# Gated linear attention and a PReLU MLP on one core: level products in pairs, keys and outputs kept in the decay tile, and a new order

## Chip, core and metric

The kernel runs on one core of a Trainium2 chip. The metric is the device time of one execution in microseconds, over several executions; the median is quoted. A profile of one further execution gives the time of every instruction. Engines are named as in the profile: PE is the matrix engine (PEld its weight loads), DVE the vector engine, ACT the scalar engine, POOL the general engine, and SP the engine whose queue issues the DMAs.

## What is computed

The input is four batches of eight heads, 768 tokens, 48 features a head. A complex decay per token and feature is limited in size, a running state of 48 x 48 per head is decayed and increased by key times value at each token, and the query reads its real part. The result goes through a two-layer MLP with a leaky activation.

```python
scale = np.minimum(mag, 0.999) / (mag + 1e-06)
a_re_n, a_im_n = (a_re * scale, a_im * scale)
for t in range(S):
    ar, ai = (a_re_n[:, :, t, :, None], a_im_n[:, :, t, :, None])
    new_re = ar * S_re - ai * S_im
    new_im = ar * S_im + ai * S_re
    S_re, S_im = (new_re + kv, new_im)
    y[:, :, t] = np.einsum('bhd,bhde->bhe', q[:, :, t], S_re)
...
h = x @ w_in                                             # 3072 x 384 by 384 x 2048
g = np.maximum(h, 0.0) + alpha * np.minimum(h, 0.0)
return (g @ w_out).astype(np.float32)
```

## The kernel before

**Units.** The attention is cut into 24 units: four batches of six chunks of 128 tokens, all eight heads at a time. The magnitudes of the decays and their phases are separated. For each unit there is a tile KQ (96 x 2 x 8 x 128: real and imaginary part of the feature on the partitions, queries and keys, heads, tokens), a tile PP of phases, and a tile T of products of decays (96 x 8 x 256). Gates (line 221 on) make phases and decays for one to three chunks at a time with long chains of DVE, ACT and POOL work, and send them to DRAM; a load brings them back in the units' layout.

**Levels.** Inside a chunk the pairs of tokens are taken in six levels, h = 1, 2, 4, 8, 16, 32: each level pairs the second half of every block of 2h tokens with its first half, and a product of queries and keys is needed for it. Between the levels a "step" (line 701) multiplies half of KQ with decays of T, in place, 1,024 elements per partition. So before each level's product, KQ stands in another state.

**One unit, in its order.** L648 multiplies KQ with the phases (2,048 elements, in place). Then, for each level: ACT copies the keys' first halves to W (L719; not for h = 1, whose keys are read with a stride), PE makes the level's product (L662: 16 small matmuls into the PSUM tile ps_lv, of which there are two), DVE steps KQ (L701), and the product is masked into a tile A (L686 on DVE for h up to 8, L683 on ACT for 16 and 32). A step may not begin before the level's product has read KQ. After the last step PE transposes the keys (L736), ACT copies them to KT (L738), PE makes the state increments (L747) and the outputs of all levels from A and the values (L759 and L768), DVE carries the state over two half chunks (L777 and L780, with decays from the last columns of T), PE adds the carried state's part to the outputs (L793), and ACT copies the outputs to yT (L807), which two DMAs (L812) write to DRAM (ysc).

**MLP.** The tokens form 14 groups of one chunk (the first two and the last two) or two chunks. For a group, xT is loaded from ysc. For each of 16 blocks of 128 hidden features PE makes three matmuls (L841), ACT and DVE apply the activation (L848 and L850), and PE adds the block to the output sum (L860, one matmul for each chunk).

**Order and queues.** Every part of the work is a generator. The string ORDER names, letter by letter, which generator goes on next (A to I gates, J to O loads and weights, P to Z and a to m the units, n and o the MLP), and each engine runs its instructions exactly in the order in which they were emitted. So PE, DVE, ACT and SP are in-order queues: an instruction that waits holds up all that stand behind it on its engine. All DMAs are issued by SP. The planner's costs in the code have no effect when the kernel is built.

**Buffers that matter here.** KQ has three buffers, PP one, T two, W two, KT one, yT one, the values V and VL one each. T of a unit comes free after the second L780 of that unit; T of the unit two later is loaded by two DMAs (L593).

Of the kernel before, what the change touches and what calls it, by code (L numbers as in the profile page):

```python
# [30 lines left out]
    "AAAAAAAAAABBAMMABMAAAAAMNAAAMMAAAAAAAAABKAAAAAAJKBBNBAKJANAAAJONNAAAAAAOBNOAAAAAAAAAAAJAAAKKAAAAAAKK"  # L31
    "KBABKLMAMKKKAAAAAAAAAAAAABBAAAAAAAAAALLLNLNOBBBBBBBBBBBBBBBOKKLJBBJBCOCNBBBBNNBBBNNNKNBBNNBBBBBOPBBO"
    "BBOOBBBBBBBLLBBBBBPCPPBBBBBBBBBBBOBJBBBBCBBBNBCBBJBPMMJBLBBBLBOPBLMLJJJPPBBCLBOBONOPBBMCCCCCPNPPCLCN"
    "CCCNNCCOPPKJCPCCJMPPJJJJPCNCOCCCCCCCCPOOOOCCCONNNPPQQCOCMCMDPPPPPPPPPPPPPPPPPNPPCNCNCCCNCPONPOCCCQCN"
    "NPKCQCCCPCPCJQQQPQQQCCCCOCCCCQCPNOJQQCOJDJPJJPPKQPDDONJDQCCCCCCCCCQCCOOCQCDQQOLOCCCCCCCDKMRnQQQMKQQK"
    "KKNCKOKOCCCCKMRJQoOCCQQQQNQoJCDQoCCOCLOCCNCCQONLoooLLLDLLDNNDLLDoooDDLoRoNLoRDoRNNDRDRooLLNRJRRDDDDD"
    "NQRoRQKoQQQRDKDJQEREoDONJDDDMDDDQooooDoDooooooRQooooooQooEDoooDoRRRRoooOooOOooooooDRRRJRoJDSooooooRD"
    "RoRRLooQQooELoSOOOLLLLLLLDDDLLLRQQQSRRKKoLDEooSoQooOoDRooRooLoSoDoooEDDooRoooRRROSRRRREoooooQRREDDDD"
    "SDDDDDDoDEESJJSJEEQDJJRJJJSKSSSTSDDLLLRRRRRRLLLESSSDLLTSDEnToTDDSTSETTSSSSLSJTSSSLLDDDDDDDDEEDDDDooS"
    "LLLoKTSooJSoEooSEoDDDDSEETSSSSSSJJSSSSETTTDJEEETDJooEEEEoUTJJJJLLoEooEEJTooDSoooooEoooTDDDTDoSSSSSoL"  # L40
    "LLLLLLooooUTooULLooEooooULJETDTooDooooooDDTDUoooTTooooLooDUoDooKLTTDooooTToooooDDDTETToUUoooTooToTTT"
    "TTnoDoooooooooTLLLUUoooKooLLLLLUTUoLooLooFEJLTUUUULoooooEoJUEooooooUUUUUUEJooEULEEooooooooUoTKEEEToo"
    "EEUVoTToTUUoEoooVVoooooEooooooVUJVVoUFoVUUooTVoUVVUVEUUJJJJUEEEEEEEEEEEEUoUJJTLTVUVFVoVoFWooFVJVVooo"
    "VFooooUUUVVVJUWVKVVUVWWoooooVLLWLLLLLWLLEEEEEEEEEEEEEEEELVVoVLLoWWoLJVVoWoVUoVWVVVooEooooJEEUWWWoVVV"
    "VWVVVVoWWJJJJJJXooEFnFooEEoEELLLLLLLLKJEFLoooVEoooEEooLEooWLLLWXoWLooooWWEoooEooooKEXEWWWKoVVooooooo"
    "KXooEooooXWJWJXXoooWooooWWFoVVoWVXWooooooWWFXFWWWFEWWFFFFGFXooLJLLLLLLXWooooooWFWFXXJFoooFooooFWoFXX"
    "oLLFoGooooJJooooooJFoWFXXXFWFFFWFFFoFooWFoXFFWXooooooFooooooooooXXXXYooooooooGJFWWFXXFXYooFFoooXLLXX"
    "LFFooooooooooLoooYXGLoooXJoooooGYXXFXXFFXXXXXFFFFFFFJYYFJnYJXoGYoooooJFFFFFFFFFFFFFFFLFJJYZFoooooooL"
    "ooGoYZYXXXGJYYZooXooZZoGoooooYooYXoFooooYYYYYYYYYZZoooZFZFFFooooFXJYZoLLLoYoYJYoLLLLLLLKYoYoYooZGLLY"
    "YKYYYYJFYZYYJKXFFFGGooYYJYLLLJLFFLoooooaFFFoYLFFFoFoJJJooZLFZYYYGYYaGLoLLoLLooooooooFLLFoFFFoooooooo"  # L50
    "ooooZoooaZaJZaoooGoZaJZnGZZZZZaooooooooooooaaooaGaZZoooaooZoJoooJGoZZooZoZoooZaHZZZGGoGGGGGGGZZZZZGZ"
    "GaZKKHLGGGoooooaGGoooooooGooobooGoaoooaoaaaaaoooLoGGbooobbZaaaoaaZooaJZZZLJoLLLLLLLLLLoGGGGaaoooGboG"
    "GJoooZaJJoabboooooooaaaaaaaaGHJZHGJJbbbbGGGLGGooooooHoooobaobJJaGGGGGGGGaaaooJJboocooooooobbcoGGbcHb"
    "ooGbLJJKooooooooooooocbGbHcHcLGLcGGKooooooLLbHbLcbbaabGGGGGGooooobbKcGbGJGJGcLLGGGooooHGGcobbbcHoooo"
    "bbLooooLLLLbbbnbcGHbbbbbJGGGdoooooGoLLoocbGGGGGccbooooJJboooGKobGGoGHooLLLLLLoooGHbbbboLooooooooGcLL"
    "LdddccccHdooooocccooooooocdcccdooJoddoLoooooHJcdocLHdJoHdHKHdcoJJooooooocccccIIccoccceooJJooHLLLoooo"
    "oooLoLdeLcHHcccHHHHccccoLLLHHLHHHHnooHoHHHLooooooooHJooooeIdLLLooooooooddooooooeeeHHHHdooHoHHdHeeooo"
    "oooooodddddeooooooodJdoJoeooHHHHHHHHHHHoodoodododeoododooodeedddddddHHdHHHHHHIeeKKeeKHJJooJfooooIooo"
    "ooeeeKeddfoLLdeeooeoeoooJooLooooddLLHHHHHHHHHHHHHHJeedIeeeLfooLLoLLooefLLLLeIofdooeeeHHeeeeeeHHefIIf"
    "IfHfJHHJHJdJooooooeeJJJJJeeeoeegLJHLHHLLofoLLLLLLLofIoooooooooIHooLJffooJoHoooooHogofHoHHIoooooIoooo"  # L60
    "noffoHHooooogfoofoooooffIffffLgoogoooofgooLoffIfJoofoIfIIooJoIfoofooooffffffffffgKggooooohLLLooLhogo"
    "oIoLgghgoooooJJILLLoooLLLffILLfhIIIgghoooooooooohgooJJhgfJJfhhKffggIgggKgooohoooohhggggJghooohoogogo"
    "IgIgooooggIgggggggIhJhoLLgLgIIIIJgIogooooKKoIoooIhooLooILhIoooooooggKJIIIIIIIIJJoooooiLIhoooIIIIoIoo"
    "oooihnooIhhhhihhiooooIiooooLLLLLLiihhLLohohoooooohohohoooohhIIIIhhIhhhhhhJJJIooooooooooJJLiioihiioio"
    "JIoLooLiiijoooooIIIooooIIIioIIIIIIIIIIoiiiiiihhhhhjLLhjLoLLLLLLLiJIIIIIIIoooooojooooojoiijjjoooiooio"
    "jiiooooiLhIIIIIoIoioiiiiiiJLLLLLILooooooLLoooiIioooiiiiiIijjoIiiiIIooooooooooooonJooJJJJooojjjjooooo"
    "ooooooooooooJoLLjjoojojjoojoLkojLjjoooooooooojjkokoooooojjkkjookkoooojjjooLooooLjkjjjjJkkooojjkjjkoo"
    "oooJoooooooookJJokjjJJLllLooLokLkoLoLLLjjkkLkkkLLLLLkkjJjjkooooooooooooJkollkokkJoooooooooookllllooj"
    "kokooJJJlJokoooookkkkJkkkkkkkkkllLLlkLLooomkkkoooolooooooLollooooolloJooomloooonoooooooooooooooooooo"
    "oooooooooollllJlmmooooooooooolmmlooooooolllooolLLLLolomLLLLLllooooooooollloolmlmmmmoooooooomlllloooo"  # L70
    "ooooooooooomlmlmlmoolommllllnoooooooooooooommLmmmoooooooooooooooooooooooooomoLomLooooomommoLLLLLoooL"
    "LLmmmLLooooooooooooooooooooooooooooooooooooooooooommmmmmmmmoommmmmoooooomnoooooooooooooooooooooooooo"
# [30 lines left out]
def kernel(  # L103
# [46 lines left out]
    LEVELS = [1 << i for i in range(6)]  # L150
# [16 lines left out]
    masks, by_row = {}, {}  # L167

    def mask(h):

        m = work.tile([P, P // h, h], F32, tag="W", name="mask", bufs=2)
        nc.gpsimd.memset(m, 1.0)
        nc.gpsimd.affine_select(out=m, in_=m, pattern=[[-h, P // h], [0, h]], base=0,
                                channel_multiplier=1, compare_op=ALU.is_ge, fill=0.0)
        nc.gpsimd.affine_select(out=m, in_=m, pattern=[[h, P // h], [0, h]], base=h - 1,
                                channel_multiplier=-1, compare_op=ALU.is_ge, fill=0.0)
        masks[h] = consts.tile([P, HC], F32, tag=f"mask{h}", name=f"mask{h}")
        flat = m.rearrange("p n h -> p (n h)")
        for i in range(2):
            nc.gpsimd.tensor_copy(masks[h][64 * i:64 * i + 64],  # L180
                                  flat[64 * i:64 * i + 64, HC * i:HC * (i + 1)])


    for h in (16, 32):
        by_row[h] = []
        for m in range(HC // h):
            t = consts.tile([P, 1], F32, tag=f"rows{h}_{m}", name=f"rows{h}_{m}")
# [8 lines left out]
    def step(*args, **kwargs):  # L196
# [5 lines left out]
        KQ=3, PP=1, T=2, V=1, W=2, KT=1, St=3, yT=1, xT=2, raw0=1, raw1=1, raw2=1, g0=0, g1=0, g2=0, ot=2, top=2,  # L202
# [7 lines left out]
    bias_tiny = consts.tile([P, 1], F32, tag="bias_tiny")  # L210
    nc.vector.memset(bias_tiny, TINY)
    bias_one = consts.tile([P, 1], F32, tag="bias_one")
    nc.vector.memset(bias_one, ONE)
    bias_two = consts.tile([P, 1], F32, tag="bias_two")
    nc.vector.memset(bias_two, 2.0)
    bias_plus = consts.tile([P, 1], F32, tag="bias_plus")
    nc.vector.memset(bias_plus, 2.0 ** -100)
    bias_half = consts.tile([P, 1], F32, tag="bias_half")
    nc.vector.memset(bias_half, -0.5)

    def gates(g, b, c0, c1):
# [136 lines left out]
        run = work.tile([P, 2, NK, GT // L // Rn + 1], F32, tag="run", name="run", bufs=2)[:, :, :, 0:nr + 1]  # L358
        ends = runs = work.tile([P, 3, NK * GT // L // Rn], F32, tag="runs", name="runs", bufs=2)[:, :, 0:rows]

        def three(dst, re_im, k, t):

            yield ACT(1.5 * k, t)
# [9 lines left out]
        t = yield from three(ends, blk[:, :, Rn - 1], 2 * rows, t)  # L373
# [18 lines left out]
        for o in range(2):  # L392
# [4 lines left out]
            tiny_engine.tensor_tensor(out=offv[:, o, 1:Rn], in0=m[:, 0], in1=m[:, 1], op=ALU.add)  # L397

# [13 lines left out]
        begin = work.tile([P, 2, NK], F32, tag="begin", name="begin", bufs=2)  # L412
# [149 lines left out]
    def loads():  # L562
        for u in range(NU):
# [24 lines left out]
            for i in range(2):  # L588
                rows = slice(i * D, (i + 1) * D)
                t = yield DMA(393, ("T", u), takes=() if i else (R["T"],))  # L590
                if i == 0:
                    L["T"] = T = work.tile([D2, H, TL], F32, tag="T", name="T", bufs=2)
# [43 lines left out]
    KT = consts.tile([P, H * D2 + P - D2], F32, tag="KT")  # L636
    nc.gpsimd.memset(KT[:, H * D2:], 0.0)
    nothing = KT.bitcast(BF16)[:, 2 * H * D2:2 * H * D2 + D]

# [3 lines left out]
    def unit(u):  # L643
        b, c = divmod(u, NCH)
        r = yield DVE(2 * H * P, ("KQ", u), ("rotation", u))
        L = loaded[u]
        KQ, PP = L["KQ"], L["PP"]
        nc.vector.tensor_tensor(out=KQ, in0=KQ, in1=bass.AP(  # L648
            tensor=PP.tensor, offset=PP.offset, ap=[PP.ap[0], (1, 2), (P + 1, H), (1, P)]), op=ALU.mult)
# [3 lines left out]
        def meet(h, weights, *after):  # L653

            e = yield PE(0.28, *after, *[("met", h, u - 1)] * (u > 0), takes=(R["lv"], R[h]), mode=1, n=16)
# [297 lines left out]
```

## Time and profile before

| what | us |
|---|---|
| median of three executions (lowest, highest) | 863.18 (861.69, 864.44) |
| the profiled execution | 859.8 |
| its span, first to last instruction | 858.1 |
| PE busy, 11,488 records | 704.7 |
| DVE busy, 996 records | 655.6 |
| ACT busy, 913 records | 427.1 |
| steps L701, 144 of 1,248 ns | 178.3 |
| phase products L648, 24 of 2,292 ns | 55.0 |
| key copies L719, 120 of 623 ns | 74.3 |
| level products L662, 4,608 records | 68.5 |
| copies to KT L738, 48 of 479 ns | 23.0 |
| copies to yT L807, 96 of 366 ns | 32.0 |

The times of the profile are those of one execution, so sums made from them are set against its own time and not against the median. Records of one engine overlap at their ends, so that the mean of one instruction is longer than what it adds to its engine's busy time. An fp32 matmul leaves two records. What bounds the end is a matter of stages, not of the totals: no engine is busy for the whole span.

### The profile page before, as it was taken

What the parts mean: (1) busy time and instruction counts of PE and PEld (TensorE: products, weight loads), DVE (VectorE), ACT (ScalarE), POOL (GpSimd) and SP (SyncE); (2) the same over time, 40 slices, a digit from 0 to 9 for tenths busy, and PEclk for the clock granted to TensorE, in tenths of its full rate; (3) what the DMA queues carried; (4) which work ended last, traced back from release to release, by engine and by line L of the source; (5) the groups of instructions that cost most, each with busy time, mean ns of one, the idle gap of its engine ahead of it and who ended that gap; (6) DMA issues with size and microseconds to landing.
All of it is one profiled execution on the core that took longest, in us unless ns stands there. A gap on an engine that the chain in (4) does not pass through costs nothing.

```text
span 858.1 us, 26855 instructions
## 1 busy us (share of the span) xinstructions
PE 704.7 (82%) x11488; PEld 529.1 (62%) x11488; DVE 655.6 (76%) x996; ACT 427.1 (50%) x913; POOL 186.3 (22%) x293
## 2 busy tenths in 40 slices
PE   0000414976898999999999999999999999999998
PEld 0000313655676777777777777777777777777776
DVE  5999999999976899789978987798867665444212
ACT  7757578576434565554555554654334234233221
POOL 5212323457313200440034005300052000000000
PEclk9999965896999999999999999999999999999999
DMA  7689977977688778669684787865674766221110
GB/s 222 170 211 232 269 175 178 241 154 154 170 194 165 159 195 207 125 135 227 160 182 110 180 216 147 158 170 127 176 155 74 173 121 134 63 51 38 39 39 9
DMA packets 194559, 130.92 MB, mean 153 GB/s; under 512 B 74504, under 2 KB 186248, under 8 KB 194440
## 3 DMA queue, kind: packets, MB, share of 16 engines
q1 hardware_dynamic: 194440, 129.20, 64.9%
q8 instruction: 90, 1.47, 0.8%
q14 instruction: 29, 0.24, 0.1%
HBM read 100.82 MB, written 35.71 MB: 159 GB/s over the span
## 4 chain that ended last, share of the span: by engine, by line
PE 74%; DVE 15%; SPq 3%; issue 3%; DMA 3%; ACT 2%; DVEq 0%; ACTq 0%
PE ps_o L860 29%; PE ps_h L841 29%; PE ps_lv L662 5%; PE ps_y L768 4%; DVE KQ L701 3%; PE ps_kv L747 3%; PE ps_y L793 3%; SPq L556 2%; DVE gate L336 2%; PE ps_kt L736 2%; DMA V<-in_v_dram 1%; DVE gate L338 1%; DVE gate L316 1%; DVE gate L296 1%; DVE gate L422 1%
## 5 line engine op out<-in xcount | busy, mean ns | idle before, releaser
L841 PE MATMUL ps_h<-xT,w_in_sb 128*128 128x256 f32 (+1 forms) x1344 | 303.4, 357 | 0.0
L860 PE MATMUL ps_o<-w_out_sb,g_sb 128*128 128x384 f32 x768 | 297.5, 501 | 7.2 <-DVE g_sb L850 7.1
L841 PEld LDWEIGHTS ps_h<-xT,w_in_sb 128*128 128x128 f32 x1344 | 233.8, 193 | 69.9 <-issue 1.7
L701 DVE TENSOR_TENSOR KQ<-KQ,T 96x1024 f32<-96x1024 f32 x144 | 178.3, 1248 | 44.1 <-PE ps_lv L662 41.1
L848 ACT ACTIVATE g_sb<-ps_h 128x256 f32<-128x256 f32 (+1 forms) x224 | 78.9, 353 | 235.8 <-PE ps_h L841 235.1
L850 DVE SCALAR_TENSOR_TENSOR g_sb<-g_sb,al,ps_h 128x256 f32<-128x256 f32 (+1 forms) x224 | 97.5, 437 | 126.8 <-ACT g_sb L848 126.4
L860 PEld LDWEIGHTS ps_o<-w_out_sb,g_sb 128*128 128x128 f32 x768 | 137.4, 192 | 58.0 <-DVE g_sb L850 9.7
L662 PE MATMUL ps_lv<-KQ,W 96*32 96x32 f32 x3840 | 56.5, 205 | 57.5 <-ACT W L719 54.1
L719 ACT COPY W<-KQ 96x512 f32<-96x512 f32 x120 | 74.3, 623 | 55.4 <-DVE KQ L701 54.1
L662 PEld LDWEIGHTS ps_lv<-KQ,W 96*32 96x32 f32 x3840 | 44.6, 116 | 83.0 <-ACT W L719 62.4
L662 PE MATMUL ps_lv<-KQ 96*32 96x32 f32 x768 | 12.0, 206 | 68.2 <-DVE KQ L648 52.6
L511 POOL TENSOR_SCALAR top<-top 128x768 f32<-128x768 f32 x16 | 43.5, 2721 | 84.3 <-ACT top L503 84.0
L648 DVE TENSOR_TENSOR KQ<-KQ,PP 96x2048 f32<-96x2048 f32 x24 | 55.0, 2292 | 0.0
L662 PEld LDWEIGHTS ps_lv<-KQ 96*32 96x32 f32 x768 | 9.5, 119 | 71.8 <-DVE KQ L648 52.6
L336 DVE TENSOR_TENSOR gate<-gate 128x576 f32<-128x576 f32 (+5 forms) x84 | 48.3, 575 | 3.1 <-ACT gate L308 1.3
L768 PE MATMUL ps_y<-A,VL 64*48 64x64 f32 x2304 | 42.2, 223 | 8.6 <-issue 6.8
L683 ACT ACTIVATE A<-ps_lv,rows 128x64 f32<-128x64 f32 x144 | 39.2, 331 | 19.4 <-PE ps_lv L662 19.0
L336 POOL TENSOR_TENSOR gate<-gate 128x72 f32<-128x72 f32 x42 | 19.0, 451 | 127.2 <-ACT gate L366 124.4
L768 PEld LDWEIGHTS ps_y<-A,VL 64*48 64x48 f32 x2304 | 39.6, 125 | 11.0 <-issue 8.9
L422 DVE TENSOR_TENSOR gate<-gate 128x1152 f32<-128x1152 f32 (+2 forms) x36 | 43.5, 1233 | 0.1
L807 ACT COPY yT<-ps_y 48x256 f32<-48x256 f32 x96 | 32.0, 366 | 21.1 <-PE ps_y L793 20.4
L686 DVE TENSOR_TENSOR A<-ps_lv,mask 128x256 f32<-128x256 f32 x96 | 39.5, 414 | 0.0
(100 smaller groups left out, 774.5 us busy)
## 6 DMA issues: line engine op xcount, KB each, us to landing
T<-decs SPq DMA_DIRECT2D x48, 384.0 KB
PP<-phs SPq DMA_DIRECT2D x48, 193.5 KB
KQ<-in_q_dram SPq DMA_DIRECT2D x48, 192.0 KB
decs<-gate SPq DMA_DIRECT2D x7, 1152.0 KB
phs<-gate SPq DMA_DIRECT2D x14, 576.0 KB
KQ<-in_k_dram SPq DMA_DIRECT2D x40, 192.0 KB
vsc<-in_v_dram SPq DMA_DIRECT2D x48, 144.0 KB
VL<-vsc SPq DMA_DIRECT2D x24, 288.0 KB
```

What stands on the lines that cost most here:

```text
L336: on(4 * k).tensor_tensor(out=m, in0=w[:, 1::-1].unsqueeze(2).to_broadcast([P, 2, 2, k]), in1=pairs_of(u), op=ALU.mult)
L422: TT(out=m[:, a], in0=U5[:, 1 + a], in1=turned(off3, o)[:, a].unsqueeze(1).unsqueeze(3).to_broadcast([P, L // 2, nb, 2]), op=ALU.mult)
L511: nc.gpsimd.tensor_scalar(out=top, in0=top, scalar1=F64_SMALL, scalar2=None, op0=ALU.max)
L648: nc.vector.tensor_tensor(out=KQ, in0=KQ, in1=bass.AP(tensor=PP.tensor, offset=PP.offset, ap=[PP.ap[0], (1, 2), (P + 1, H), (1, P)]), op=A ...
L662: nc.tensor.matmul(t[64 * i + j:64 * i + j + HC // 2, p], lhsT=weights(4 * i + p)[:, j:j + HC // 2], rhs=q_[:, m * g:m * (g + 1)], start=T ...
L701: nc.vector.tensor_tensor(out=x, in0=x, in1=m, op=ALU.mult)
L719: nc.scalar.copy(W.rearrange("p n t -> p (n t)").rearrange("p (m h) -> p m h", h=h), halves(KQ[:, 1].rearrange("p n t -> p (n t)"), h)[:, ...
L768: nc.tensor.matmul(o, lhsT=Vp[h][64 * i:64 * i + 64, s, e_ * D:(e_ + 1) * D], rhs=a, start=False, stop=False)
L841: nc.tensor.matmul(p, lhsT=w_in_sb[:, f // 2, kk, f % 2 * P:(f % 2 + 1) * P], rhs=x_of[m][:, kk], start=(kk == 0), stop=(kk == NK - 1))
L848: nc.scalar.activation(gt, p, AF.Relu, scale=-1.0)
L850: nc.vector.scalar_tensor_tensor(out=gt, in0=gt, scalar=al_1[:, f:f + 1], in1=p, op0=ALU.mult, op1=ALU.add)
L860: nc.tensor.matmul(sums[0], lhsT=gt[:, c * P:(c + 1) * P], rhs=w_out_sb[:, f], start=(f == 0), stop=(f == NF - 1))
```

## The change

**Pairs.** The levels are visited in pairs (1, 2), (4, 8), (16, 32). The first level of a pair is made from a copy of both its halves, queries' and keys' (tile WQ, of which there are two), so that its step waits for the copy and no longer for the product. For h = 1 there is no extra copy: the phase product is split in two of 1,024 elements, and the one for the half concerned writes straight into WQ (L665 of the changed kernel), from which step 1 then writes KQ. For h = 4 and 16 ACT copies 1,024 elements (L744). For h = 2 and 8 ACT copies the keys as before; for h = 32 the keys are read in place. Both products of a pair go into one PSUM tile, and the two masks follow after the second step of the pair.

**Tiles.** KT and yT are gone. T has 128 partitions; its first 128 columns, done with after step 1, take the transposed keys (two copies each, the second one filling the gap from column 96 to 128), and after the state increments the outputs. T therefore comes free when the outputs of the unit have been written to DRAM. The small constant columns share one tile, a small zero tile takes the place of KT's zero columns, and some buffers of the gates (run, runs, begin) are single instead of double.

**Order.** ORDER is new as a whole.

```diff
-    LEVELS = [1 << i for i in range(6)]
+    VISITS = [(1, 2), (4, 8), (16, 32)]
+    LEVELS = [h for visit in VISITS for h in visit]
...
-        r = yield DVE(2 * H * P, ("KQ", u), ("rotation", u))
...
-        nc.vector.tensor_tensor(out=KQ, in0=KQ, in1=bass.AP(
-            tensor=PP.tensor, offset=PP.offset, ap=[PP.ap[0], (1, 2), (P + 1, H), (1, P)]), op=ALU.mult)
+        def some(at, q_to_k):
+
+            return bass.AP(tensor=KQ.tensor, offset=KQ.offset + at, ap=[KQ.ap[0], (H * P + q_to_k, 2), (P, H), (2, HC)])
+
+        def phases(at, q_to_k):
+
+            return bass.AP(tensor=PP.tensor, offset=PP.offset + at, ap=[PP.ap[0], (q_to_k, 2), (P + 1, H), (2, HC)])
+
+        first_slot = spare.pop(0)
+        WQ = work.tile([D2, 2, H, HC], F32, tag=f"WQ{first_slot}", name="WQ", bufs=1)
+        nc.vector.tensor_tensor(out=WQ, in0=some(1, -1), in1=phases(1, 0), op=ALU.mult)
+        r = yield DVE(H * P)
+        nc.vector.tensor_tensor(out=some(0, 1), in0=some(0, 1), in1=phases(0, 2), op=ALU.mult)
...
-        def meet(h, weights, *after):
-
-            e = yield PE(0.28, *after, *[("met", h, u - 1)] * (u > 0), takes=(R["lv"], R[h]), mode=1, n=16)
-            t = ps.tile([P, HP, HC // 2], F32, tag="lv", name="ps_lv", bufs=2)
+        def meet(h, shared, at, keys, queries, *after, takes=()):
+
+            e = yield PE(0.28, *after, *[("met", h, u - 1)] * (u > 0), takes=takes, mode=1, n=16)
+            if not shared:
+                shared.append(ps.tile([P, 2, HP, HC // 2], F32, tag="lv", name="ps_lv", bufs=2))
+            t = shared[0][:, at]
...
-        for h in LEVELS:
-            w = k_
-            if h == 1:
-                weights = lambda n: KQ[:, 1, n].rearrange("p (m s) -> p m s", s=2)[:, :, 0]
-            else:
-                w = yield ACT(H * HC, k_, takes=(R["W"],))
-                W = work.tile([D2, H, HC], F32, tag="W", name="W", bufs=2)
...
-            e, t = yield from meet(h, weights, w, k_)
...
-            k_ = yield DVE(2 * H * HC, e, *[("decays", u)] * (h == 1))
-            T = L["T"]
-            step(h)
-            yield from mask_out(h, t, e)
+        for visit in VISITS:
+            ready = []
+            for h in visit:
...
+                elif h != visit[-1]:
+                    held = "WQ"
+                    w = yield ACT(2 * H * HC, k_, takes=(R[held],))
+                    slot = spare.pop(0)
+                    z = work.tile([D2, 2, H, HC], F32, tag=f"WQ{slot}", name="WQ", bufs=1)
+                    nc.scalar.copy(z.rearrange("p i n t -> p i (n t)").rearrange("p i (m h) -> p m i h", h=h), bass.AP(
+                        tensor=KQ.tensor, offset=KQ.offset + h, ap=[KQ.ap[0], (2 * h, H * HC // h), (H * P - h, 2), (1, h)]))
...
+                if h != visit[-1]:
+                    k_ = yield DVE(2 * H * HC, w, *[("decays", u)] * (h == 1))
+                    T = L["T"]
+                    step(h, WQ if h == 1 else None)
+            tiles, shared = [], []
+            for at, (h, keys, queries, held, slot, w) in enumerate(ready):
+                e = yield from meet(h, shared, at, keys, queries, w, k_, takes=() if at else (R["lv"],))
...
+            if visit[-1] != 1:
+                k_ = yield DVE(2 * H * HC, e)
+                step(visit[-1])
+            for h, ta, e in tiles:
+                e = yield from mask_out(h, ta, e)
...
-            nc.scalar.copy(KT[:, 4 * i * D2:4 * (i + 1) * D2].rearrange("p (n d) -> p n d", n=HP), t)
+            nc.scalar.copy(T[:, 4 * i:4 * (i + 1), 0:D2], t)
+            nc.scalar.copy(T[:, 4 * i:4 * (i + 1), D2:P], t[:, :, 0:P - D2])
...
-        R["T"].put(k_)
...
-                    yT = work.tile([P, 2, 2, P], F32, tag="yT", name="yT", bufs=1)
+                    yT = T[:, 0:4, 0:P].rearrange("p (i s) t -> p i s t", i=2)
...
-                              yT[64 * e_:64 * e_ + D].rearrange("p i s t -> p (i s) t"))
-        R["yT"].put(t)
+                              T[64 * e_:64 * e_ + D, 0:4, 0:P])
+        R["T"].put(t)
```

## The prediction

> **What bounds the kernel now.** I read the page's totals and 40 slices first, then the windows by stage, then who waited for whom, then the timeline of one level product. The slices show two regimes:
>
> ```profile
> PE 704.7 (82%) x11488; PEld 529.1 (62%) x11488; DVE 655.6 (76%) x996; ACT 427.1 (50%) x913; POOL 186.3 (22%) x293
> ...
> PE   0000414976898999999999999999999999999998
> ...
> DVE  5999999999976899789978987798867665444212
> ...
> PEclk9999965896999999999999999999999999999999
> ```
>
> A slice is 21.5 us. DVE is full from the second slice to the eleventh while PE fills; from about the fourteenth on PE is full. The windows put numbers on it (columns: length, busy time and instructions of PE, PEld, DVE, ACT, POOL, granted clock, DMA share, GB/s):
>
> ```profile
> 141.00:205.00 64.00, 45.73 (x945) 34.62 (x945) 62.75 (x88) 42.96 (x79) 34.06 (x33) 0.77 0.75 180
> 205.00:250.00 45.00, 39.17 (x788) 29.98 (x787) 38.86 (x59) 17.96 (x49) 12.46 (x18) 0.94 0.80 187
> 250.00:307.00 57.00, 52.84 (x961) 40.34 (x959) 46.25 (x59) 31.21 (x76) 15.49 (x34) 0.97 0.79 158
> ...
> 360.00:858.00 498.00, 493.91 (x7353) 367.37 (x7351) 335.04 (x470) 208.75 (x507) 74.86 (x140) 1.00 0.56 125
> ```
>
> Up to 205 us DVE sets the pace, after 307 PE does, and in the 102 us between neither is full: DVE idles 17. Its waits there (from 205 to 307: us, times, longest), and what PE waits for meanwhile:
>
> ```profile
> DVE g_sb L850 <- ACT g_sb L848: 7.8, 6, 3.7
> DVE KQ L701 <- PE ps_lv L662: 7.2, 4, 4.0
> ```
>
> ```profile
> PE ps_y L768 <- issue: 6.0, 3, 2.7
> ```
>
> Over the whole run DVE waits 41.1 us for level products, but 33.1 of it after 307, where DVE has time to spare. So the change is not worth 41 us.
>
> A ledger of the two queues follows. Both engines run their instructions in a fixed order. I gave each DVE instruction the time its kind adds to DVE's busy time here (a 1,024-element step 1.19 us net of overlap), and each matmul its spacing, start to start, between 300 and 858 us (L860 0.653, L841 0.436 for two chunks and 0.222 for one, a transpose 0.166, a level product 0.0165, ps_kv 0.030, ps_y 0.027, a carried-state product 0.054, plus the changes of array tile priced below). Summed in the built order of both kernels, up to the first eviction (L850) of a token group on DVE, and from the group's first L841 to the end on PE:
>
> ```
> point            DVE queue ahead     PE work left       sum
>                  before   after     before   after     before   after
> group 0           126.6   136.2      670.4   659.3      797.0   795.5
> group 1           191.0   183.9      633.6   629.7      824.6   813.6
> group 2           229.7   217.8      600.4   600.9      830.1   818.7
> middle of 2       254.4   244.7      577.0   576.4      831.4   821.1
> group 3           276.7   271.4      552.6   551.4      829.3   822.8
> middle of 3       301.9   298.9      526.2   526.4      828.1   825.3
> group 4           321.4   323.4      498.6   493.9      820.0   817.3
> ```
>
> In the trace of before those evictions end at 140.6, 205.0, 249.8, 281.6, 307.2, 332.8 and 358.4 us: DVE is behind its queue by 14.0, 14.0, 20.1, 27.2, 30.5, 30.9 and 37.0 us. Time plus PE work left at the middle of group 2 is 281.6 + 577.0 = 858.6, the span (858.1): that is where PE becomes the bound. The end is therefore a sum of the ledger plus DVE's lag at its binding point.
>
> [...]L841 to L841 is 0.218 us, L841 to L662 0.306 (+0.09); L662 to L662 0.008, L662 to L841 0.126 (+0.118). [...]Here xT waits from 819.4 to 821.7 us for ysc, 2.3 us.
>
> ```profile
> 540.43 0.59 PE L841 MATMUL ps_h<-xT,w_in_sb 128*128 128x256 f32 x2
> 540.96 0.46 PE L662 MATMUL ps_lv<-KQ,W 96*32 96x32 f32 x32
> 541.35 1.13 PE L841 MATMUL ps_h<-xT,w_in_sb 128*128 128x256 f32 x4
> ```
>
> **The change part by part.**
>
> *PE.* The same 5,984 products. Changes of array tile fall from 262 to 199 (98 separate stretches of level products become 67; not every pair stays together). 63 x 0.11 = 6.9 us less, 679.1 to 672.2. The ledger shows that little of it is left as such: after has 7.0 us less PE work before the middle of group 3 and as much after it.
>
> *DVE.* The 2,048-element phase product (2,292 ns) becomes two of 1,024. Net of overlap 2 x 1.21 - 2.21 = 0.21 us a unit, 5 us in 24 units; three or so of these units lie before group 2. Steps and masks keep their sizes. The order outweighs it: group 0 is reached 9.6 us later, group 1 7.1, group 2 11.9, group 3 5.3, the middle of 3 only 3.0 us earlier. So the binding point moves to the middle of group 3.
>
> *The levels' chain.* Before, steps 1 to 32 each wait for a product. Now steps 2, 8 and 32 do; 1, 4 and 16 wait for DVE or for an ACT copy. The 7.2 us of level waits between 205 and 307 I halve: -3.6. An ACT copy of 1,024 was not run: the 512 one takes 623 ns and one of 1,152 takes 1,259, so about 1.1[...], against 0.62. Copies per unit: 5 x 0.62 = 3.1 before; 2 x 1.1 + 2 x 0.62 = 3.4 now. Behind a late copy stand its step on DVE and then its product on PE, and the products queued behind that.
>
> *Transposed keys into T.* Two copies a unit (479 ns) become two plus two of 128 elements (0.27 to 0.37 by the 277 to 366 rows): +0.6 us. ACT goes from 427 to about 455, busiest where it had 43 of 64 us: hidden there, at most 1 us a unit on the chain into ps_kv if not.
>
> *T held longer.* Before, T is free for unit u+2 after the carried states; now only when the outputs of u, copied into it, are in DRAM. SP issues T(u+2) behind that wait, and every later load of SP stands behind it. The loop from unit u's last carried-state product to the second level product of u+2: four copies 1.25, ysc issue and landing 0.5 + 2.3, two T issues 0.9, T's packets 5.5 after the second issue (median here, 3.8 to 7.4), step 1.2, copy 0.6[...]: 13.0, plus 0.6 for each DMA that SP issues in between. PE work queued in that stretch is the cover. It is short at unit 6 (12.7 against 16.6), about even at 3 (15.9, 16.0) and 9 (20.1, 20.8), 1 to 2 over at 7, 8 and 22, and 2 to 11 over elsewhere. Unit 6 lies in the binding stretch: +3.5. Constant columns and the zero tile are set once: nothing. The single run buffers I take at nothing too; at most a small gate step (0.2 to 0.6 us) waits in each of eight gates.
>
> *Sum.* Lag at the middle of 3: 27.2 of before, + 3.0 because DVE and PE have to run together for one more group before PE takes over (27.2 rose by 3.3 over the like stretch), + 3.5 for T, - 3.6 level waits, - 4.1 for the greater part of the 7.0 us of PE work that no longer stands in the mixed stretch (bounds 0 and 7): 26.0. 825.3 + 26.0 = 851.3, 6.8 below the span of 858.1. The profiled execution took 859.8, so 853.0 of that kind; the median of before is 863.18, 3.4 above it, which gives 856.4. I say 857.
>
> **Rivals.**
>
> *The lag stays small (0.14).* If crossed waits of level chain and MLP caused most of it, the lag stays at 14 plus 4: 843.3, median 848. For it: it is 14.0 up to group 1. Against: half the waits between are evictions waiting for ACT, and PE stalls for values (6.0), which are not touched.
>
> *No change (0.13).* The lag at the middle of 3 is before's 30.9 or a little more: 856.2 to 858.5, median 861 to 864. For it: at equal lag the sums there differ by 2.8 us only.
>
> *T's longer hold decides: slower (0.27).* If the loop takes 2.5 us longer than summed (a 1.3 us DVE or ACT instruction ahead at each end), it is short by 16 us in all, at units 3, 6, 7, 8, 9, 12, 13, 16 and 22; 3.5 are in my sum already, so +12.5: 863.8, median 869. PE's order is fixed, so it waits at the second level product with MLP work behind it. It outweighs the gain from about 1.8 us extra. For it: before had T(u+2) issued ahead of ysc(u) for most units (163.2 against 178.8 at unit 3, 247.2 against 265.7 at unit 6). Against: PE's real spacing before 300 us is wider than its work.
>
> *Products not really paired:* 14 stretches still hold one level; counted above.
>
> **How the numbers follow.** Forecast 0.46, 850 to 860; small lag 0.14; no change 0.13; slower 0.27. A measurement here tells 0.3% (2.6 us) from nothing. Faster 0.60, same 0.13, slower 0.27. The range 845 to 872 leaves out half of the fast case and the far end of the slow one.
>
> **What would show it.** Right: PE full from about 330 us, group 2's first eviction near 235, DVE waits for level products at half of 41.1, changes of tile as counted, waits for T at unit 6 only. Wrong: PE waiting for steps or copies after 330 us in stretches of over 1 us at second level products, with a T load issued less than 8 us before; or a lag over 33 us at the middle of group 3.

## The result and the profile after

| | before | after |
|---|---|---|
| median of seven executions, us (lowest, highest) | 862.57 (858.61, 864.85) | 856.40 (851.62, 858.58) |
| the profiled execution, us | 859.8 | 853.84 |
| its span, us | 858.1 | 851.8 |

The ratio of after to before is 0.9928, 95% interval 0.9909 to 0.9948: 6 us faster, at 856.4 us where 857 were forecast. A second measurement of the same kernel gave 855.86 us and a ratio of 0.9931 (0.9906 to 0.9957), with a span of 855.9 in its profile. The two together are 0.9929, give or take 0.0016, and the experiments are compared with that. Executions of the changed kernel at a granted clock of 0.98 or more (five of the sixteen) have a mean of 853.5 us and the other eleven one of 857.3, and the experiments hold different shares of the two, so that differences of 2 us between them tell little.

The page after, totals and slices (a slice is 21.3 us):

```profile
PE 697.3 (82%) x11488; PEld 530.0 (62%) x11488; DVE 653.9 (77%) x1020; ACT 439.5 (52%) x937; POOL 206.6 (24%) x293
...
PE   0001414776998899899999999999999999999998
...
DVE  5999999997997899599989986987776756633212
...
PEclk9999656798999999999999999999999999999999
```

PE is at 9 throughout only from the eighteenth slice on, where it was from the fourteenth: three eights stand in the thirteenth, fourteenth and seventeenth. Up to 360 us PE is busy 210.8 us before and 210.4 after, so PE is not fuller in the early part as a whole; it has less to do, 7.4 us less busy time (6.3 in the second profile). Its idle time is no shorter: span less busy time is 153.4 us before, 154.5 and 157.5 after. DVE has 1.7 us less busy time. The windows after, in the stretches of the prediction (length, busy time of PE, PEld, DVE, ACT, POOL, granted clock, DMA share, GB/s):

```profile
141.00:205.00 64.00, 45.88 (x847) 36.11 (x842) 60.56 (x86) 44.10 (x86) 37.32 (x40) 0.87 0.72 176
205.00:250.00 45.00, 43.25 (x865) 34.41 (x865) 38.88 (x61) 20.27 (x49) 11.29 (x11) 0.95 0.73 179
250.00:307.00 57.00, 51.62 (x969) 39.56 (x965) 49.48 (x67) 36.56 (x84) 27.30 (x35) 0.97 0.69 138
307.00:360.00 53.00, 49.18 (x860) 36.84 (x859) 41.49 (x63) 23.67 (x52) 7.56 (x22) 0.97 0.81 191
360.00:851.80 491.80, 486.95 (x7269) 365.90 (x7267) 335.93 (x484) 215.37 (x519) 80.68 (x140) 1.00 0.56 129
```

PE has 94.9 us of work between 205 and 307, where it had 92.0 before. DVE idles 13.6 us there, against 16.9 before, and between 307 and 360 PE still has gaps of 3.8 us. DVE's waits from 205 to 307 us (total, times, longest) are others now:

```profile
DVE g_sb L902 <- ACT g_sb L900: 3.9, 4, 1.6
DVE KQ L721 <- DMA T<-decs: 3.8, 2, 2.5
DVE KQ L721 <- ACT WQ L744: 3.0, 2, 2.6
DVE St L833 <- PE ps_kv L801: 2.8, 1, 2.8
```

The waits for level products, 7.2 us here before, are gone altogether. In their place stand waits for T's load, for the ACT copy of 1,024 and for the state products. Over the whole run DVE waits 25.1 us for level products (41.1 before), all of it after 307 us. The chain of waits from 180 to 262 us names T's load as well; these are its DMA pieces (start, us):

```profile
187.22 3.39 DMA ysc<-T
190.68 5.56 DMA T<-decs
219.39 7.44 DMA T<-decs
255.98 7.68 DMA T<-decs
```

These are the loads of T for units 4, 5 and 6, 20.7 us of the chain in 82. The first stands directly behind the store of unit 2's outputs. In the second profile the chain names the loads of units 5 and 6 there. The chain of the kernel before has no load of T at all.

Ends of the first evictions of a group on DVE, with the lag (the end less the ledger's DVE queue) in brackets:

```
point         ledger   forecast  after          after, 2nd run  before
group 0       136.2              147.7 (11.5)   147.7 (11.5)    140.6 (14.0)
group 1       183.9              197.5 (13.6)   197.1 (13.2)    205.0 (14.0)
group 2       217.8     235      236.6 (18.8)   235.7 (17.9)    249.8 (20.1)
middle of 2   244.7              266.5 (21.8)   267.5 (22.8)    281.6 (27.2)
group 3       271.4              296.5 (25.1)   298.8 (27.4)    307.2 (30.5)
middle of 3   298.9    324.9     323.1 (24.2)   325.4 (26.5)    332.8 (30.9)
group 4       323.4              356.4 (33.0)   360.0 (36.6)    358.4 (37.0)
```

Behind group 4 the comparison is simple, because PE is full there in both kernels. The traces show the same products left on PE from that eviction on (2,816 records of level products in both, 16 fewer short records of ps_y after), and 213 changes of array tile against 250 before. This last stretch takes 499.7 us before, 495.4 and 495.9 after. So 4.3 and 3.8 us of the shorter spans (6.3 and 2.2) arise behind group 4; the group itself is reached 2.0 us earlier in one profile and 1.6 later in the other.

### The profile page after: what moved, and what is told of

The parts are those of the page before. It is cut to its first block, busy times and chain, and to the rows that moved or that the text cites. A ratio compares the mean times of both kernels' runs of the same rounds, so it can differ in the third digit from the quotient of the medians.

```text
span 851.8 us, 26881 instructions
## 1 busy us (share of the span) xinstructions
PE 697.3 (82%) x11488; PEld 530.0 (62%) x11488; DVE 653.9 (77%) x1020; ACT 439.5 (52%) x937; POOL 206.6 (24%) x293
## 4 chain that ended last, share of the span: by engine, by line
PE 58%; DVE 25%; DMA 7%; issue 3%; ACT 3%; SPq 3%; POOL 1%; DVEq 0%; ACTq 0%; POOLq 0%
PE ps_o L912 23%; PE ps_h L893 22%; DVE KQ L721 5%; PE ps_lv L682 4%; DVE gate L339 4%; DMA T<-decs 3%; PE ps_y L821 3%; DVE gate L427 2%; DVE gate L341 2%; PE ps_y L845 2%; PE ps_kv L801 2%; SPq L630 1%; DVE g_sb L902 1%; PE ps_kt L789 1%; DVE gate L430 1%
## 5 line engine op out<-in xcount | busy, mean ns | idle before, releaser
L721 DVE TENSOR_TENSOR KQ<-KQ,T 96x1024 f32<-96x1024 f32 x120 | 147.3, 1231 | 31.5 <-PE ps_lv L682 25.1
L682 PE MATMUL ps_lv<-WQ 96*32 96x32 f32 x2304 | 34.7, 204 | 79.3 <-DVE WQ L665 51.9
L682 PEld LDWEIGHTS ps_lv<-WQ 96*32 96x32 f32 x2304 | 26.8, 116 | 97.0 <-DVE WQ L665 51.9
L744 ACT COPY WQ<-KQ 96x1024 f32<-96x1024 f32 x48 | 50.0, 1042 | 14.9 <-DVE KQ L721 14.8
L760 ACT COPY W<-KQ 96x512 f32<-96x512 f32 x48 | 30.8, 642 | 43.7 <-DVE KQ L721 37.3
L859 ACT COPY T<-ps_y 48x256 f32<-48x256 f32 x96 | 30.8, 366 | 38.9 <-PE ps_y L845 38.3
L789 PE MATMUL ps_kt<-ident,KQ 96*128 96x96 f32 x192 | 26.4, 263 | 22.3 <-DVE KQ L721 12.2
L703 ACT ACTIVATE A<-ps_lv,columns 128x64 f32<-128x64 f32 x144 | 37.3, 336 | 13.0 <-PE ps_lv L682 12.8
L789 PEld LDWEIGHTS ps_kt<-ident,KQ 96*128 96x128 f32 x192 | 22.3, 150 | 30.9 <-ACT T L792 10.9
L801 PEld LDWEIGHTS ps_kv<-V,T 64*64 64x64 f32 x1408 | 28.0, 148 | 15.4 <-ACT T L792 8.7
```

Source lines behind the costliest of these rows:

```text
L682: nc.tensor.matmul(t[64 * i + j:64 * i + j + HC // 2, p], lhsT=keys(n, g), rhs=queries(n, g), start=True, stop=True)
L721: nc.vector.tensor_tensor(out=x, in0=x if x0 is None else x0, in1=m, op=ALU.mult)
L744: nc.scalar.copy(z.rearrange("p i n t -> p i (n t)").rearrange("p i (m h) -> p m i h", h=h), bass.AP(tensor=KQ.tensor, offset=KQ.offset + ...
L789: nc.tensor.transpose(t[:, p], KQ[:, 1, 4 * i + p], ident[:D2, :D2])
L801: nc.tensor.matmul(kv[s][j:j + HC, n], lhsT=T[rows, n, j:j + HC], rhs=V[rows, n // 2, (n % 2) * D:(n % 2 + 1) * D], start=True, stop=True)
```

## The experiments

Each ratio is to the kernel before, with its 95% interval.

**T freed early.** The outputs go to the unit's own KQ tile:

```diff
-            KQ = work.tile([D2, 2, H, P], F32, tag="KQ", name="KQ", bufs=3)
+            KQ_all = work.tile([P, 2, H, P], F32, tag="KQ", name="KQ", bufs=3)
+            KQ = KQ_all[0:D2]
...
-                    yT = T[:, 0:4, 0:P].rearrange("p (i s) t -> p i s t", i=2)
+                    yT = L["all"][:, 1, 0:4].rearrange("p (i s) t -> p i s t", i=2)
...
-                              T[64 * e_:64 * e_ + D, 0:4, 0:P])
+                              L["all"][64 * e_:64 * e_ + D, 1, 0:4])
```

> The changed kernel with its outputs copied into the unit's own KQ tile (its key half, done with after the transposes; KQ of the unit three later is loaded after them anyway) instead of T. T of a unit is free again after the state's decays, as before the change, and the load of T two units later no longer waits for the outputs to land in DRAM (2.3 us), though it stays at its place in SP's queue. Theory A (the hold costs what my sum says, 3.5 us at unit 6, and about as much at unit 4): the T loads of units 4 and 6 start about 2.3 us earlier, the waits of L721 for T (6.0 us in 3) fall to under 2, and the time is 2 to 5 us below the changed kernel's 856.4: ratio to the kernel before 0.987 to 0.991. Rival B (the hold is hidden, another chain is as late): waits for T fall but the time stays within 1 us, ratio 0.992 to 0.994. Rival C (the hold is the largest loss, over 8 us): ratio below 0.984.

Measured: 854.91 us, ratio 0.9915 (0.9889 to 0.9941), 1.2 us below the changed kernel with an uncertainty of 2.6. It can't be told from no gain. The waits for T only fell from 6.0 to 4.7 us, where under 2 was expected, and the lag, 15.6 at group 2 and 18.8 at its middle, is back at 23.7 at the middle of 3. The next run adds the place in the queue. A part of ORDER around unit 4's output stores (T), with the two J that issue T of unit 6:

```diff
-UVUoTUTVooUEEoooEULLLLLoooUUUJJJF
+UVUoJJTUTVooUEEoooEULLLLLoooUUUJF
```

> As the run with outputs in KQ, and in nine units (3, 5, 6, 8, 9, 11, 16, 17 and 18) the two issues of T's load also stand ahead of the output stores of the unit two before in SP's queue instead of behind them. Theory A: the early ones of these (units 5 and 6) get T a further 4 us or more sooner; a further 1 to 3 us fall away in all, ratio 0.984 to 0.990; units 16 to 18 give nothing since PE is the bound there. Rival B: no further gain, 0.991 to 0.994. Rival D: the loads that now wait for the release of T or for the decays hold up the output stores behind them and so the groups' xT: slower than the run with outputs in KQ by 1 us or more.

Measured: 846.88 us, ratio 0.9824 (0.9798 to 0.9850): 9.1 us below the changed kernel, uncertainty 2.6 (the two intervals put together); taken separately above and below a granted clock of 0.98, the means differ by 6.9 and 9.5 us. SP's queue shows why. After, around unit 4's stores (start, us, line, tiles, count):

```profile
251.03 1.44 SPq L864 DMA_DIRECT2D ysc<-T  x2
252.56 0.40 SPq L726 DMA_DIRECT2D St<-in_v_dram  x1
253.02 1.91 SPq L630 DMA_DIRECT2D VL<-in_v_dram  x4
254.97 0.43 SPq L633 DMA_DIRECT2D VL<-vsc  x1
255.51 0.94 SPq L598 DMA_DIRECT2D T<-decs  x2
```

and with the load moved:

```profile
243.47 3.46 SPq L631 DMA_DIRECT2D VL<-in_v_dram  x5
247.04 1.75 SPq L599 DMA_DIRECT2D T<-decs  x2
248.89 0.90 SPq L865 DMA_DIRECT2D ysc<-KQ  x2
```

T of unit 6 is issued 8.5 us earlier, 6.3 of them against the first of the stores; freeing T alone left it behind six other DMAs. DVE's waits from 205 to 360 us in this run hold no wait for T any more, where the kernel after has 6.0 us:

```profile
DVE KQ L722 <- PE ps_lv L683: 8.2, 5, 3.2
DVE g_sb L903 <- ACT g_sb L901: 4.4, 6, 1.4
DVE KQ L722 <- ACT WQ L745: 3.5, 3, 2.6
DVE St L834 <- PE ps_kv L802: 0.2, 1, 0.2
```

The lags of this run's profile are 14.6, 14.7, 15.3, 19.4 and 20.4 us at group 1, group 2, the middle of 2, group 3 and the middle of 3. So they stay near 15 up to the middle of group 2, where after they have grown to 21.8. Up to there the growth came from T.

Only the loads of units 5 and 6 moved:

> Outputs in the unit's KQ tile, as in the first run of this kind, and only the loads of T for units 5 and 6 put ahead of the output stores of units 3 and 4, instead of nine such loads. Theory A (the late T counts where DVE is still the bound, to about 307 us, so at units 5 and 6): most of the gain of the run with nine early loads, 5 us or more below the run with outputs in KQ alone: ratio 0.982 to 0.987. Rival (every late T counts a little, or the loads of units 8, 9 and 11 decide): under 3 us of it, ratio 0.988 to 0.992.

Measured: 850.46 us, ratio 0.9878 (0.9840 to 0.9916), 3.2 us below the run with outputs in KQ alone, with an uncertainty of 4. That lies between both expectations: by the times these two loads make up some two fifths of what the nine add. By the lags they make up nearly all of it: 16.0 us at the middle of 2, 21.8 at the middle of 3 and 27.7 at group 4, where the run with nine early loads has 15.3, 20.4 and 27.1. What the other seven give stays open.

**Where DVE time counts.** One instruction more per unit, in six units:

```diff
                     step(h, WQ if h == 1 else None)
+                    if h == 1 and 0 <= u < 6:
+                        t_ = T[0:D2, :, 0:P]
+                        nc.vector.tensor_tensor(out=t_, in0=t_, in1=t_, op=ALU.max)
```

> The changed kernel with one more DVE instruction of 96 x 1,024 (the larger of T's first 128 columns and themselves, right after step 1, when these columns are done with) in each of units 0 to 5: 6 x 1.21 = 7.3 us of DVE work ahead of the middle of group 3. Theory A (two regimes, DVE the bound up to about 307 us, PE after): nearly all of it arrives at the end, 5.5 to 7.5 us more than 856.4: 862 to 864, ratio 0.999 to 1.002. Rival (PE bounds throughout, DVE's lag is only crossed waits, so DVE has room): under 2 us more, ratio under 0.995.

> The same additional DVE instruction in units 14 to 19 instead (480 to 670 us), also 7.3 us. Theory A: hidden, within 1 us of 856.4, ratio 0.992 to 0.994. Rival (the chain of steps and products within a unit counts at every place): 3 to 7 us more, ratio 0.996 to 1.001.

Measured: early 861.87 us, ratio 1.0019 (1.0002 to 1.0036), 7.8 us slower than the changed kernel for 7.3 us of work. Late 859.09, ratio 0.9959 (0.9945 to 0.9973), 2.6 us slower, uncertainty 1.8. The two regimes stand. The late one may not hide everything: the estimate is about a third, and the stretch from group 5 to group 13 takes 415.5 us against 412.7 and 413.4 in the two profiles of the changed kernel. That is a weak sign, since the four other runs with the same late work on PE and DVE (outputs in KQ, the two runs with early loads, early DVE work) take 412.7 to 414.2. No single wait of PE carries it: between 480 and 690 us PE waits 1.0 us there, and 0.9 in the changed kernel's second profile.

**What a change of array tile costs.** For 26 pairs of units 10 to 23 one neighbouring matmul of the MLP (o) goes between the two products, as here for unit 10 (Z):

```diff
-ooZYYZYYZGYYZZoY
+ooZYYZYYoZGYYZZY
```

> The changed kernel in which, for 26 pairs of level products in units 10 to 23 that stand side by side on PE, the one neighbouring matmul of the MLP (L893 or L912) goes between the two products. Nothing is added and no other engine's order changes; 52 more changes between kinds of matmul (360 instead of 308), all after some 360 us. Theory A (a change costs 0.09 to 0.12 us of PE's time, and PE is the bound there): 52 x 0.105 = 5.5 us, 4.5 to 6.5 slower than the changed kernel, ratio 0.998 to 1.002. Rival (changes hide behind the weight loads, and the run with all first products moved was slow for its waits alone): under 2 us, ratio under 0.9955.

Measured: 863.35 us, ratio 1.0007 (0.9988 to 1.0025), 6.7 us slower than the changed kernel, uncertainty 2.1. It is the same work with 52 more changes, each 0.13 us (0.09 to 0.17). The stretch from group 5 to 13 takes 419.9 us in its profile, 6.5 to 7.2 more, while PE's idle time (156.8 us) lies between those of the two profiles after. Late on PE, then, the price of a change is paid in full, and the rival is out. At this price the 37 changes that the changed kernel saves behind group 4 are worth 4.8 us by estimate; 4.3 and 3.8 were measured.

**What the pairs save.** First the first product of each pair goes ahead of its step, which it still doesn't hold up:

```diff
                     T = L["T"]
+                    meet(h, shared, 0, keys, queries)
                     step(h, WQ if h == 1 else None)
...
-                e = yield from meet(h, shared, at, keys, queries, w, k_, takes=() if at else (R["lv"],))
+                e = yield PE(0.28, w)
+                if at:
+                    meet(h, shared, at, keys, queries)
```

> The changed kernel with the first product of each pair moved on PE from behind the pair's second copy to just ahead of its step; it still reads the copy, so the step doesn't wait for it. Nothing else moves. The two products of a pair now stand apart: 117 stretches of level products on PE instead of 67 (100 of one level instead of 14), 98 more changes between kinds of matmul. Theory A (a change of array tile costs 0.09 to 0.12 us also where PE is the bound): 98 x 0.105 = 10.3 us more PE work, about two thirds of it after 300 us: 5 to 10 us slower than the changed kernel, ratio 0.999 to 1.004. Rival (the changes hide in PE's queue, or the earlier products give back what they cost): within 2 us of the changed kernel, ratio under 0.996.

Then this product also reads KQ in place, so that the step has to wait for it:

```diff
-        nc.vector.tensor_tensor(out=WQ, in0=some(1, -1), in1=phases(1, 0), op=ALU.mult)
+        nc.vector.tensor_tensor(out=some(1, -1), in0=some(1, -1), in1=phases(1, 0), op=ALU.mult)
...
+                    def queries(n, g, h=h):
+                        m = HC // (2 * h)
+                        return halves(KQ[:, 0, n], h)[:, :, 1][:, m * g:m * (g + 1)]
```

> As the run with the products apart, but the first product of each pair reads its queries (for h = 1 its keys too) from KQ in place, and the phase product for that half writes into KQ, so that steps 1, 4 and 16 wait for a product again, as all steps did before the change. Copies, their sizes and PE's order are those of the run with the products apart; the copied queries of h = 4 and 16 are not used. Theory A (a wait for a product costs only while DVE is the bound, up to about 307 us): 2 to 5 us slower than the run with the products apart; DVE's wait for level products back to 35 to 50 us over the run, most of it after 307. Rival D (the chain inside the unit was never late): within 1 us of it. Rival E (the waits are what the pairs save, at every place): 8 us or more slower than it.

Measured: 907.31 us, ratio 1.0512 (1.0485 to 1.0538), and 932.99 us, ratio 1.0835 (1.0800 to 1.0869). Both are far beyond what either side expected. The first is 50 us slower than the changed kernel; 98 changes of tile at the 0.13 us measured above explain some 13 of them by estimate. PE idles 181.6 us, 27 more than after, and its waits show the product's place in this. PE's waits for the copies in the changed kernel,

```profile
PE ps_lv L682 <- ACT WQ L744: 27.4, 4, 9.0
PE ps_lv L682 <- ACT W L760: 14.2, 7, 3.7
```

and with the products moved up:

```profile
PE ps_lv L681 <- ACT WQ L741: 40.1, 18, 7.6
PE ps_lv L681 <- ACT W L757: 15.6, 8, 3.5
...
PE ps_lv L681 <- issue: 11.0, 6, 3.6
...
PE ps_lv L681 <- DVE gate L339: 9.5, 1, 9.5
```

Directly behind its copy, a product is met by PE before the copy is done, with MLP work queued behind it: 4 waits become 18. The waits for W hardly change; those for a gate and those put to "issue" are new at level products. Some 10 of the 50 us are left over. The product also takes its PSUM tile earlier, and there are two of these; what that costs was not measured. So this run measures the order on PE more than the changes of tile, which is why these were priced alone above. The second run, in the same order, adds 28 us by the ratios. DVE's waits for level products in the first and then in the second:

```profile
DVE KQ L718 <- PE ps_lv L681: 36.4, 27, 4.0
```

```profile
DVE KQ L717 <- PE ps_lv L680: 82.1, 72, 3.0
```

Rival E is the one that the number supports, but not its "at every place": the two profiles reach group 5 at 435.5 and 435.3 us, and 22.6 us between them arise from there to group 13, where theory A expected nothing. In this order PE is not full there (113.4 of the 120 us from 360 on in the first run); what the waits would cost in the order of after can't be taken from it. Old waits in the new order, with the products apart, make a far slower kernel than before. The pairs in the old order were not run, so that the shares of the pairs and of the order in the whole gain stay open.

**The gap in T.** The two gap copies go; POOL writes zeros, first right after step 1, then just ahead of step 32:

```diff
+                        nc.gpsimd.memset(T[:, :, D2:P], 0.0)
...
-            nc.scalar.copy(T[:, 4 * i:4 * (i + 1), D2:P], t[:, :, 0:P - D2])
```

> The changed kernel with the two copies of 128 elements that fill the gap in T beside the transposed keys (48 in all, 279 ns, 13.4 us of ACT) left out and the gap zeroed by POOL right after step 1, once for each unit; the gap's products are read by nothing. Theory A (the copies cost at most some 0.3 us on the chain into the state products, where PE waits for them in 3 places): 0 to 2 us faster than the changed kernel, ratio 0.990 to 0.994. Rival (ACT's added work delays activations in the stretch that binds): 3 us or more faster. Rival F (POOL stands in its gate chain and comes late with the zeros): slower, with PE waiting for POOL ahead of the state products.

> The gap in T zeroed by POOL as in the run before with such zeros, but issued just ahead of step 32 instead of right after step 1, so that POOL meets it when step 1 is long done. The 48 ACT copies of 128 elements are left out as there. Theory A (that run was slow because POOL waited for step 1 with the gates' work behind it): POOL's waits ahead of T, 191 us there, are nearly gone, and the time is 0 to 2 us below the changed kernel: ratio 0.990 to 0.994. Rival (zeros on POOL are themselves late or disturb DVE): still slower than the changed kernel by over 3 us, ratio over 0.996.

Measured: 870.02 us, ratio 1.0098 (1.0068 to 1.0128), then 856.55 us, ratio 0.9948 (0.9934 to 0.9963). The first is 15 us slower than the changed kernel though the zeros take 0.31 us each. POOL's longest wait in it:

```profile
POOL T L769 <- DVE KQ L721: 191.5, 15, 41.6
```

and in the second:

```profile
POOL T L780 <- DVE KQ L721: 64.0, 5, 31.7
```

POOL stood before step 1 with the gates' work queued behind it: the gates' last store of decays is issued at 610.2 us, 588.3 after. The first eviction of group 1 came 4.3 us later than after (201.8). Rival F holds for that run, with the gates late rather than the zeros: of PE's waits of 2.8 us or more in all none is for POOL. Issued later the loss is gone, though a third of the waiting is not, and no gain shows (1.6 us slower, uncertainty 1.9): the gap copies cost nothing that can be measured.

**Together.**

> Outputs in KQ, nine early loads of T, and the zeros on POOL just ahead of step 32 in place of the 48 ACT copies: what the runs so far suggest together. Theory A: as the run with nine early loads (ratio 0.9824) or up to 2 us faster, 0.979 to 0.983. Rival (zeros on POOL disturb): over 0.985.

Measured: 851.40 us, ratio 0.9876 (0.9852 to 0.9900), 4.5 us slower than with the nine early loads alone, uncertainty 3. By themselves the zeros cost 1.6 us (uncertainty 1.9); the difference is within the two uncertainties. Up to group 4 this run is ahead of the one with nine early loads alone (348.1 against 350.5 us); from there to the end it takes 502.0 us against 497.9. Why isn't settled. The kernel that beats both is the one with outputs in KQ and nine early loads of T, 846.88 us. The changed kernel itself once more:

> The changed kernel itself once more, beside the others of this group, so that differences of 2 us can be read. Both theories: ratio to the kernel before 0.992 to 0.995, as in the first measurement (0.9928).

Measured: 855.86 us, ratio 0.9931, told of above.

## Why the prediction came out, step by step

*The ledger and the lag* gave the right total. The lag at the middle of group 3 was forecast at 26.0 and measured at 24.2 and 26.5; the span at 851.3 and measured at 851.8 and 855.9. But the binding point lies later than I said. By the ledger the middle of 3 gives 849.5 and 851.8 for the end, group 4 (356.4 + 493.9 and 360.0 + 493.9) gives 850.3 and 853.9, the largest of the points in both profiles. PE still has gaps up to 360 us, so PE is full some 30 us later than the 330 that I gave. That early DVE work counts in full was shown by adding it.

*But the lag was put together wrongly, and two errors cancelled, so that it is partly luck that the total fits.*

The term for T was too small, and too narrow. I had "+3.5", at unit 6 only. Undoing the hold and the late issue gains 9.1 us, uncertainty 2.6. DVE's three waits for T after stand at units 5, 6 and 9 (1.3, 2.5 and 2.2 us), and I had put unit 5 among those with cover to spare. I had counted the loop and the DMAs in between, which is the right mechanism. (0.7 of the loop's 13.0 us, for the hand-overs from one engine to the next, was my estimate; in the trace of before such a hand-over takes 0.03 us at the median from L701 to L719, 0.05 from L793 to L807 and from L719 to L662, and 0.14 from L662 to L701.) I then compared it with the PE work queued in that stretch as if a loop that is just covered cost nothing. The early loads show that it did: the lag fell by 3 to 8 us from group 2 on, at the middle of 3 by 3.8 and 6.1. It is the cause that the slower rival named ("T's longer hold decides"), at a little over half its size: 9.1 us where that case has 3.5 + 12.5.

The other terms came out too large. Without T, my sum for the middle of group 3 is 22.5; the run with early loads has 20.4. The "7.2 us of level waits" that I halved to 3.6 went to zero; over the whole run 25.1 of 41.1 us are left, where I said half. That run's 846.88 us lies beside the rival *the lag stays small* (848), which I had refused because the waits for ACT and the PE stalls are "not touched". All the same the waits of DVE for ACT's activations between 205 and 307 fell from 7.8 us to 3.9, and those of PE at ps_y from 6.0 to 2.0. These last I called stalls for values, where the profile puts them to "issue" and names no releaser.

*Changes of tile*: the stretches of level products fall from 98 to 67 as counted, and a change costs 0.13 us late on PE (0.09 to 0.17) where I had 0.11. But my "little of it is left as such" rests on the middle of 3, where PE's work left is 0.2 us apart. At group 4, where PE is full in both kernels, the ledger's own line has 4.7 us less PE work after, and the traces 4.3 and 3.8. So the changes saved late bring most of what the two profiles gain. (The 5,984 products of the prediction are 5,888, counted from the records: 192 transposes and 96 bf16 products with one record each, the other 5,600 with two; no sum rests on it.)

*DVE and ACT.* The groups after (columns: busy, mean ns, idle before):

```profile
L721 DVE TENSOR_TENSOR KQ<-KQ,T 96x1024 f32<-96x1024 f32 x120 | 147.3, 1231 | 31.5 <-PE ps_lv L682 25.1 <-ACT WQ L744 6.0
...
L744 ACT COPY WQ<-KQ 96x1024 f32<-96x1024 f32 x48 | 50.0, 1042 | 14.9 <-DVE KQ L721 14.8
...
L667 DVE TENSOR_TENSOR KQ<-KQ,PP 96x1024 f32<-96x1024 f32 x24 | 30.2, 1258 | 0.2
L665 DVE TENSOR_TENSOR WQ<-KQ,PP 96x1024 f32<-96x1024 f32 x24 | 29.6, 1231 | 0.0
...
L792 ACT COPY T<-ps_kt 128x128 f32<-128x128 f32 x48 | 13.4, 279 | 0.0
```

The two phase products take 59.8 us where the one took 55.0: +4.8, as forecast (+5). The copy of 1,024 takes 1,042 ns, where I had estimated about 1.1 us from the copies of 512 and 1,152 in the trace of before. ACT's total is 439.5 and not 455, of no consequence. The gap copies take 0.28 us each and are hidden, as priced.

*The slower rival* had 0.27. The hold cost 5.6 us more than my term, nearly the 6.8 us of gain that I had summed; the kernel was still faster only because the rest gained more. That PE's spacing before 300 us is wider than its work, my reason against this rival, did not protect it.

*Taken at nothing and not tested*: the gates' single buffers and the shared constants.

## What to carry to other kernels

When a tile is kept longer to save room, look at where its next load stands in the issuing queue: here freeing the tile was worth nothing that could be measured, freeing it and issuing its load ahead of the stores was worth 9.1 us. A sum that hits the total may still be built of terms that cancel; undo the doubtful one before you believe it. Compare two kernels from the point on where the same engine is full in both: there 37 fewer changes of tile showed as 4 us, while at a point 33 us earlier the sums seemed to say that they bring nothing. And an instruction of 0.31 us, once a unit on an engine with time to spare, cost 15 us here when it waited at the head of the queue.

## What the hardware showed unexpectedly

- A change of array tile cost 0.13 us on a full PE (0.09 to 0.17), which agrees with the 0.09 and 0.118 read from the spacings of neighbouring records of the kernel before. Between L841 and L860, which both show 128*128, records there start 0.216 us apart at the median past 360 us, as between two of L841.
- 7.3 us of DVE work laid where PE was busy for over 99% of the time still cost 2.6 us (uncertainty 1.8), though all waits of PE that the profile shows between 480 and 690 us come to 1.0 us.
- PE waits that the profile puts down to nothing visible ("issue"), 0.8 to 4.5 us each, stand between 270 and 350 us in five profiles of this order: after, outputs in KQ, nine early loads, and DVE work early and late (2.0 and 2.5 us after, ending at 290.9 and 344.7). Soon after the two in the profile after, the granted clock is 0.5 for 3.4 us each (from 291.3 and from 345.9). In the later of these stretches the records of the carried-state products (L845) start 53 ns apart on average, where they start 28.5 apart between 420 and 470 us at a clock of 1.00. If the waits and the lower clock belong together, which was not shown, they cost more than their idle time. The waits are a part of the loss between 280 and 360 us, and what makes PE idle there wasn't found.
- The granted clock is 0.5 from 93.4 to 144.6 us in the profile after, and 0.956 over the run (0.953 in the second profile). The profile of the run with two early loads has 0.986 over the run. The 0.014 that it lacks of full clock comes to 11.8 us of its 845.8, less than half of the 25.6 us that a stretch like that one takes, so there is none in it. Executions of the changed kernel with a mean clock of 0.98 or more were nearly 4 us faster (853.5 against 857.3).
